# RWKV attention with a top-1 router: attention in halves of 64 rows, both products of R as one moving operand

## The chip, the cores and the metric

One core of a Trainium2 chip. The metric is the device time of one launch in microseconds (us), the median of the runs.

## The reference

Attention (4 sequences, 8 heads, 768 steps, width 48), step by step, and then a router that sends each of 3072 tokens to the best of 8 experts:

```
for t in range(S):
    cur = u * k_t (outer) v_t
    y_t = r_t @ (state + cur)
    state = w * state + k_t (outer) v_t
x = y as [3072, 384];  logits = norm(x) @ norm(emb).T / tau
e = argmax(logits);    gate = softmax(logits)[e]
out = gate * (relu(x @ w1[e]) @ w2[e])          # float32 throughout
```

## The kernel before, in words

The attention is worked in chunks of 128 steps, two sequences at a time: 6 chunks x 2 pairs of sequences = 12 *turns* (t = 0 to 11; `c, bp = divmod(t, 2)`). After the turns come the experts, one after the other, which the change does not touch except for the names of two PSUM banks.

In a chunk K and R are scaled by powers of w that grow and fall with the row (`scale_k`, `scale_r`, GpSimd). TensorE turns them so that the width lies on partitions (`turn_in`, L304) and ScalarE copies them out of PSUM (`take_in`, L308: tiles KT, RT). `scores` (L318) multiplies 128 rows of K with 128 rows of R for each of 16 heads (8 heads, 2 sequences, u = 0 and 1; `par` is the head's parity and chooses a bank and 64 of the 128 partitions). VectorE multiplies with a triangle (`mask`, L350: tile AT). The diagonal carries the extra factor u: GpSimd makes KT times u (`own_k`, L286: tile KuT), TensorE makes the diagonal blocks of 64 x 64 from it (`own_scores`, L333) and VectorE writes their diagonals into AT (`own_terms`, L342). `outer` (L363) adds the chunk's K and V to the state (`next_state` L375, `decay_state` L381 on GpSimd). One turn later `with_state` (L399) and `with_v` (L412) make Y, ScalarE takes it out (`take_y`), TensorE turns it (`turn_y`, L427), ScalarE copies X out of PSUM, stores it by DMA and sums its squares.

Each second turn a chunk of four sequences is complete, and its routing follows as the *lists' steps*: `logits` (L453, TensorE), `take_logits` (lgT), `turn_logits`, `keep_logits` (lg), `choose` (L490 to L503, VectorE, with the norms' powers by GpSimd, L482), `exps`, `ranks` (TensorE), `places`, `gate`, `places_b` (tiles HV, QV, P on VectorE, L553 to L564), `put` (L572, TensorE) and `collect` (lists). The experts gather their rows by these lists.

All engines take their instructions in order. The order is written by hand: `attention` gives each step a planned time, `plan.at(time, step)`, and the steps are emitted in the order of these times. PERIOD is the planned length of a turn, 11.2; the times set only the order. PSUM has 8 banks: ps0 to ps3 (`k.D`), po0 and po1 (`k.O`), py0 and py1 (`k.Y`). The line that ties GpSimd's product to the scores is in `own_k`: `after(k, ins, k.scored)`.

Of the kernel before, what the change touches and what calls it, by code (L numbers as in the profile page):

```python
# [19 lines left out]
C = 128  # L20
NCH = S // C
# [12 lines left out]
PERIOD = 11.2  # L34
# [33 lines left out]
def build_first(k):  # L68
# [23 lines left out]
    step = k.AT[1][:, 0, 0].rearrange("q (p i) -> q p i", p=NP)  # L92
    seed = k.AT[1][:, 0, 1].rearrange("q (p i) -> q p i", p=NP)
# [18 lines left out]
    for src, dst, bank in ((kp, k.kpow, k.O[0]), (rp, k.rpow, k.O[1])):  # L112
# [27 lines left out]
def build_consts(k):  # L140
# [8 lines left out]
    k.dmask = k.aconst.tile([128, DP], I32, name="dmask")  # L149
    for s in range(2):  # L150
        q = slice(s * DP, (s + 1) * DP)
        nc.vector.tensor_copy(k.dmask[q, :], k.ident[q, q])
# [73 lines left out]
def rings(k):  # L226
# [54 lines left out]
def scale_r(k, t, u):  # L281
    k.nc.gpsimd.tensor_mul(of(k.Rw, t)[:, u, :, 0:D], of(k.R, t)[:, u], k.rpow)  # L282


def own_k(k, t, u):
    ins = k.nc.gpsimd.tensor_mul(  # L286
        of(k.KuT, t)[:, u], of(k.KT, t)[:, u], k.uw[:, :, None].to_broadcast([128, NP, C])
    )
    if u == 0:
        after(k, ins, k.scored)  # L290
# [16 lines left out]
def take_in(k, t, u, which):  # L307
    k.nc.scalar.copy(  # L308
        of(k.KT if which else k.RT, t)[:, u], k.turned[u][which].rearrange("q (p i) -> q p i", p=NP)
    )  # L310


def scores(k, t, u):
    RT, KT = of(k.RT, t), of(k.KT, t)
    for p in range(NP):
        for par in range(2):
            rows = slice(par * DP, par * DP + D)
            k.scored = k.nc.tensor.matmul(  # L318
                k.D[2 * u + par][:, p * C : (p + 1) * C], KT[rows, u, p, :], RT[rows, u, p, :],
                start=True, stop=True, skip_group_check=True,  # L320
            )


def own_scores(k, t):

    RT, KuT = of(k.RT, t), of(k.KuT, t)
    for u in range(2):
        for p in range(NP):
            for s in range(2):
                for par in range(2):  # L330
                    rows, half = slice(par * DP, par * DP + D), slice(s * DP, (s + 1) * DP)
                    col = (u * NP + p) * DP
                    k.nc.tensor.matmul(  # L333
                        k.O[par][half, col : col + DP], KuT[rows, u, p, half], RT[rows, u, p, half],
                        start=True, stop=True, skip_group_check=True,
                    )
# [12 lines left out]
def mask(k, t, u, par):
    k.nc.vector.tensor_mul(  # L350
        of(k.AT, t)[:, u, par].rearrange("q (p i) -> q p i", p=NP),
        k.D[2 * u + par].rearrange("q (p i) -> q p i", p=NP),
        k.umask[:, None, :].to_broadcast([128, NP, C]),
    )


def outer(k, t):
    Kw, V = of(k.Kw, t), of(k.V, t)
    for u in range(2):
        for p in range(NP):  # L360
            for par in range(2):
                h, col = 2 * p + par, (u * NP + p) * D
                k.nc.tensor.matmul(  # L363
                    k.sums[par * DP : (par + 1) * DP, col : col + D], Kw[:, u, h, :], V[:, u, h, 0:D],
                    start=True, stop=True, skip_group_check=True,
                )


def next_state(k, t):
    c, bp = divmod(t, 2)  # L370
    new = k.sums[:, 0 : 2 * NP * D].rearrange("q (u p d) -> q u p d", u=2, p=NP)
    if c == 0:
# [11 lines left out]
def y_out(k, par, p, u):  # L384
    col = (u * 2 + p % 2) * C
    return k.Y[par][(p // 2) * DP : (p // 2 + 1) * DP, col : col + C]


def with_state(k, t):
    c, bp = divmod(t, 2)  # L390
    if c == 0:
        return
    RT, T = of(k.RT, t), k.T[bp][c % 2]
    for u in range(2):
        for q in range(2):
            for p in (q, q + 2):
                for par in range(2):
                    rows = slice(par * DP, par * DP + D)
                    k.nc.tensor.matmul(  # L399
                        y_out(k, par, p, u)[0:D], T[rows, u, p, :], RT[rows, u, p, :],  # L400
                        start=u == 0 and q == 0, stop=False, skip_group_check=True,
                    )


def with_v(k, t):
    c, bp = divmod(t, 2)
    AT, V = of(k.AT, t), of(k.V, t)
    for u in range(2):
        for q in range(2):
            for par in range(2):  # L410
                for p in (q, q + 2):
                    k.nc.tensor.matmul(  # L412
                        y_out(k, par, p, u), V[:, u, 2 * p + par, :], AT[:, u, par, p * C : (p + 1) * C],
                        start=c == 0 and u == 0 and q == 0, stop=True, skip_group_check=True,
                    )
# [153 lines left out]
def put(k, c):  # L569
    out = k.Y[1][:, 128 : 128 + 2 * E * TM]  # L570
# [6 lines left out]
def collect(k, c):  # L577
    new = k.Y[1][:, 128 : 128 + 2 * E * TM].rearrange("q (x j t) -> q x j t", x=E, j=2)
# [7 lines left out]
def attention(k):  # L586
# [3 lines left out]
    for t in range(TURNS):  # L590
# [459 lines left out]
```

## Time and profile before

| | |
|---|---|
| median of 3 runs | 560.61 us (560.07 to 563.74) |
| the profiled execution | 561.12 us, its span 559.3 us |
| TensorE granted clock, mean | 0.951 |
| TensorE busy | 502.6 us (90%), 3755 instructions |
| VectorE, ScalarE, GpSimd busy | 154.1, 103.5, 158.8 us |

The profile is of one execution; times are us from the start of its span. A float32 matmul shows as two records, so 16 matmuls are x32. PE is TensorE's matmuls, PEld its weight loads, DVE VectorE, ACT ScalarE, POOL GpSimd, SP the queue that issues most DMAs. A granted clock of 1.00 is TensorE's upper level (2.4 GHz), 0.50 the lower (1.2 GHz).

### The profile page before, as it was taken

The numbers are of one execution on the slowest core, as the hardware profiler recorded it, in microseconds if no ns is written. First come the engines' busy times: TensorE is split into PE (matmuls) and PEld (weight loads), VectorE is DVE, ScalarE is ACT, GpSimd is POOL, SyncE is SP. The second block draws the span as 40 slices with busy tenths as digits, with TensorE's granted clock in tenths as the row PEclk, the third lists the DMA queues.
The fourth block names the chain that finished last, engine by engine and source line by source line (L and its number), as shares of the span: only waits on it lengthen the run. The fifth ranks groups of instructions, "written<-read, shape, count | busy, mean of one in ns | idle before, by whom it ended". The sixth has DMA issues, their size and how long they took to land.

```text
span 559.3 us, 9057 instructions
## 1 busy us (share of the span) xinstructions
PE 502.6 (90%) x3755; PEld 316.6 (57%) x3755; DVE 154.1 (28%) x352; ACT 103.5 (19%) x223; POOL 158.8 (28%) x191
## 2 busy tenths in 40 slices
PE   7588998989897389999999999999999999999990
PEld 3487787878776244554554554554554554554550
DVE  6545667685772310200200110110110110100001
ACT  1123444333342102002002002002002102101100
POOL 5545656465640360130131031022013010020010
PEclk9788999999996679999999999999999999999996
DMA  8925579995000130341332322313314313010010
GB/s 170 198 50 124 116 163 253 281 233 125 31 31 28 51 100 0 128 142 41 128 112 76 128 88 93 127 57 129 126 34 154 113 42 113 0 44 0 0 41 8
DMA packets 95510, 54.20 MB, mean 97 GB/s; under 512 B 78781, under 2 KB 90110, under 8 KB 95458
## 3 DMA queue, kind: packets, MB, share of 16 engines
q1 hardware_dynamic: 88658, 43.67, 28.2%
q0 software_dynamic: 4096, 9.45, 4.7%
q10 hardware_dynamic: 2704, 0.40, 0.4%
q8 instruction: 31, 0.51, 0.4%
q14 instruction: 21, 0.17, 0.1%
HBM read 45.63 MB, written 11.01 MB: 101 GB/s over the span
## 4 chain that ended last, share of the span: by engine, by line
PE 77%; POOL 7%; DVE 6%; issue 3%; ACT 1%; DMA 1%; POOLq 0%; ACTq 0%; DVEq 0%
PE ps L706 30%; PE po L717 30%; POOL KuT L286 4%; PE ps L318 4%; PE py L412 3%; PE ps L304 2%; DVE AT L342 2%; PE py L697 2%; PE py L572 1%; PE po L333 1%; PE py L453 1%; PE ps L363 1%; DVE xTe L698 1%; POOL Rw L282 1%; POOL Kw L278 1%
## 5 line engine op out<-in xcount | busy, mean ns | idle before, releaser
L706 PE MATMUL ps<-xTe,w 128*128 128x512 f32 x384 | 167.9, 597 | 0.0
L717 PE MATMUL po<-w,hT 128*128 128x384 f32 x512 | 166.4, 486 | 0.0
L717 PEld LDWEIGHTS po<-w,hT 128*128 128x128 f32 x512 | 96.7, 190 | 66.2 <-issue 0.5
L706 PEld LDWEIGHTS ps<-xTe,w 128*128 128x128 f32 x384 | 73.6, 192 | 91.0 <-issue 89.1
L723 POOL DMA_INDIRECT out_dram<-y,take x32 | 31.7, 991 | 281.7 <-DVE y L722 277.5
L709 ACT ACTIVATE hT<-ps 128x512 f32<-128x512 f32 x64 | 38.2, 597 | 300.4 <-PE ps L706 300.4
L722 DVE TENSOR_SCALAR y<-po,lists 128x384 f32<-128x384 f32 x32 | 19.8, 618 | 165.5 <-PE po L717 165.5
L698 DVE COPY xTe<-py 128x512 f32<-128x512 f32 x24 | 15.9, 689 | 153.2 <-PE py L697 153.1
L286 POOL TENSOR_TENSOR KuT<-KT,uw 128x512 f32<-128x512 f32 x24 | 24.5, 1040 | 64.6 <-PE ps L318 61.1
L342 DVE COPY_PREDICATED AT<-dmask,po 64x512 f32<-64x512 int32 x48 | 35.4, 738 | 17.3 <-PE po L333 16.6
L684 POOL DMA_INDIRECT G<-xs,take x32 | 32.6, 1018 | 15.3 <-issue 8.2
L350 DVE TENSOR_TENSOR AT<-ps,umask 128x512 f32<-128x512 f32 x48 | 29.8, 683 | 15.8 <-PE ps L318 15.8
L318 PE MATMUL ps<-RT,KT 48*128 48x128 f32 x384 | 25.1, 281 | 3.0 <-ACT X L431 2.8
L412 PE MATMUL py<-AT,V 128*64 128x128 f32 x384 | 26.6, 297 | 0.0
L419 ACT COPY YT<-py 128x512 f32<-128x512 f32 x24 | 12.9, 589 | 71.0 <-PE py L412 71.0
L318 PEld LDWEIGHTS ps<-RT,KT 48*128 48x128 f32 x384 | 22.8, 190 | 5.6 <-ACT X L431 4.4
L282 POOL TENSOR_TENSOR Rw<-R,rpow 128x384 f32<-128x384 f32 x24 | 24.2, 1007 | 6.1 <-DVE wC L118 5.8
L333 PE MATMUL po<-RT,KuT 48*64 48x64 f32 x768 | 16.7, 224 | 9.8 <-POOL KuT L286 9.8
L278 POOL TENSOR_TENSOR Kw<-K,kpow 128x384 f32<-128x384 f32 x24 | 24.2, 1008 | 0.0
L412 PEld LDWEIGHTS py<-AT,V 128*64 128x64 f32 x384 | 23.5, 150 | 1.1 <-issue 0.4
L697 PE MATMUL py<-ident,G 128*128 128x128 f32 x96 | 15.6, 298 | 8.0 <-DMA G<-xs,take 5.5
L333 PEld LDWEIGHTS po<-RT,KuT 48*64 48x64 f32 x768 | 13.4, 134 | 14.3 <-POOL KuT L286 14.3
(145 smaller groups left out, 339.3 us busy)
## 6 DMA issues: line engine op xcount, KB each, us to landing
w<-in_moe_w_dram SPq DMA_DIRECT2D x24, 512.0 KB, 5.2
w<-in_moe_w_dram SPq DMA_DIRECT2D x32, 384.0 KB, 4.0
K<-in_k_dram SPq DMA_DIRECT2D x24, 192.0 KB, 3.7
V<-in_v_dram SPq DMA_DIRECT2D x24, 192.0 KB, 4.1
xs<-X SPq DMA_DIRECT2D x24, 192.0 KB, 2.0
R<-in_r_dram SPq DMA_DIRECT2D x22, 192.0 KB, 4.0
G<-xs,take POOLq DMA_INDIRECT x32, 3.4
out_dram<-y,take POOLq DMA_INDIRECT x32, 2.6
```

Source lines behind the costliest of these rows:

```text
L278: k.nc.gpsimd.tensor_mul(of(k.Kw, t)[:, u, :, 0:D], of(k.K, t)[:, u], k.kpow)
L286: ins = k.nc.gpsimd.tensor_mul(of(k.KuT, t)[:, u], of(k.KT, t)[:, u], k.uw[:, :, None].to_broadcast([128, NP, C]))
L318: k.scored = k.nc.tensor.matmul(k.D[2 * u + par][:, p * C : (p + 1) * C], KT[rows, u, p, :], RT[rows, u, p, :], start=True, stop=True, ski ...
L333: k.nc.tensor.matmul(k.O[par][half, col : col + DP], KuT[rows, u, p, half], RT[rows, u, p, half], start=True, stop=True, skip_group_check= ...
L342: k.nc.vector.copy_predicated(of(k.AT, t)[half, :, par].rearrange("q u (p i) -> q u p i", p=NP)[:, :, :, half], k.dmask[half, None, None, ...
L350: k.nc.vector.tensor_mul(of(k.AT, t)[:, u, par].rearrange("q (p i) -> q p i", p=NP), k.D[2 * u + par].rearrange("q (p i) -> q p i", p=NP), ...
L412: k.nc.tensor.matmul(y_out(k, par, p, u), V[:, u, 2 * p + par, :], AT[:, u, par, p * C : (p + 1) * C], start=c == 0 and u == 0 and q == 0, ...
L684: k.nc.gpsimd.indirect_dma_start(out=G[:, :], out_offset=None, in_=k.xs[:, :], in_offset=IndirectOffsetOnAxis(ap=k.take[:, e, t : t + 1], ...
L706: k.nc.tensor.matmul(ps, w1[:, m, f * 128 : (f + 1) * 128], xT[:, m, :], start=(m == 0), stop=(m == NK - 1))
L709: k.nc.scalar.activation(hT[:, f, :], ps, ACT.Relu)
L717: k.nc.tensor.matmul(ps, hT[:, f, t * 128 : (t + 1) * 128], w2[:, f, :], start=(f == 0), stop=(f == NF - 1))
L723: k.nc.gpsimd.indirect_dma_start(out=k.out[:, :], out_offset=IndirectOffsetOnAxis(ap=k.take[:, e, t : t + 1], axis=0), in_=y[:, :], in_off ...
```

## The change

The chunk of 128 stays for the scaling and the turning in, but scores, diagonal and state are worked in two halves s of 64 rows:

- RT has two parts side by side for each half: R (copied by ScalarE as before) and R times u (`own_r`, VectorE, reads the turned R in PSUM). `scores` multiplies a half of K (64 columns of weights) with the 128 columns [R, R times u] of the same half: 32 matmuls on four tiles of 64 x 64. `own_k` and `own_scores` are gone, and KuT with them.
- `mask` and `own_terms` read the two parts of one result: 4 instructions of 128x256 each instead of 4 of 128x512 and 4 of 64x512.
- `outer` gives the sums of both halves (32 matmuls, banks pu0 and pu1, which were po0 and po1); `half_state` makes the state in the middle of the chunk (tile Tmid), `next_state` the one at its end.
- Y is made by `with_v` in two phases of 16 matmuls of 64x64 and by `with_state` with 32 matmuls of 64 columns, the second half of them with Tmid. In the first phase row half s writes bank s, in the second bank 1-s; `between` (two copies of one column by ScalarE) stands before the second.
- `scale_r` of turn t+1 now has the tie to the scores of turn t that `own_k` had.
- X is turned through pu0 and pu1; the small results of the lists' steps move from py1 to columns 384 to 511 of these banks. The lists' steps are spread over one turn more, and PERIOD is 9.4.

```diff
+HC = C // 2
-PERIOD = 11.2
+PERIOD = 9.4
 def scale_r(k, t, u):
-    k.nc.gpsimd.tensor_mul(of(k.Rw, t)[:, u, :, 0:D], of(k.R, t)[:, u], k.rpow)
-def own_k(k, t, u):
...
-    if u == 0:
+    ins = k.nc.gpsimd.tensor_mul(of(k.Rw, t)[:, u, :, 0:D], of(k.R, t)[:, u], k.rpow)
+    if t and u == 0:
         after(k, ins, k.scored)
...
+def own_r(k, t, u):
+    k.nc.vector.tensor_mul(
+        of(k.RT, t)[:, u, :, :, 1, :], k.turned[u][0].rearrange("q (p s i) -> q p s i", p=NP, s=2),
+        k.uw[:, :, None, None].to_broadcast([128, NP, 2, HC]),
+    )
 def scores(k, t, u):
...
+        for s in range(2):
+            for par in range(2):
...
+                    k.D[2 * u + par][halves(s), p * C : (p + 1) * C], KT[rows, u, p, halves(s)],
+                    RT[rows, u, p, s].rearrange("q j i -> q (j i)"),
...
+def half_state(k, t):
...
+        k.nc.vector.tensor_add(k.T1[bp], k.T[bp][c % 2], added(k, 0))
 def next_state(k, t):
...
+    k.nc.vector.tensor_add(k.T[bp][(c + 1) % 2], k.T1[bp], added(k, 1))
...
+def between(k, t):
+    for par in range(2):
+        col = (1 - par) * HC
+        k.nc.scalar.copy(k.peek[:, par : par + 1], k.Y[par][:, col : col + 1])
+def with_v(k, t, phase):
...
+                for s in range(2):
+                    par = s if phase == 0 else 1 - s
...
+            plan.at(then + 4.65, keep_logits, k, c)
...
+            plan.at(then + 4.65, placed, k, c)
...
+                plan.at(then + 8.8, places_b, k, c)
+                plan.at(then + P + 1.77, put, k, c)
...
-    plan.at(6.2, build_embeddings, k)
+    plan.at(6.6, build_embeddings, k)
```

Three places show how the order moves. The first is TensorE in a turn that has `put`, from the scores to the second turning in, before (turn 6): rows of one kind show the first of them only.

```order
L318 MATMUL ps_58<-RT_118,KT_121 128x128
L399 MATMUL py_64<-RT_120,T_1_132 48x128
L333 MATMUL po_62<-RT_118,KuT_122 64x64
L412 MATMUL py_64<-AT_123,V_110 64x128 x2
L363 MATMUL ps_58<-V_112,Kw_116 64x48 x16
L304 MATMUL ps_59<-ident,Rw_102 128x128 x4
```

and in the changed kernel (turn 7; `put` is L596, `with_v` L414, `with_state` L433, `outer` L363):

```order
L328 MATMUL ps_60<-RT_119,KT_121 64x128 [waits DVE_49,Activation_49]
L596 MATMUL pu_63<-QV,P 128x64 [waits DVE_49,Activation_49]
L414 MATMUL py_64<-AT_122,V_110 64x64
L433 MATMUL py_64<-RT_118,T_1_131 48x64
L302 MATMUL ps_58<-ident,Rw_102 128x128 [waits DVE_49,Pool_49]
L414 MATMUL py_65<-AT_122,V_110 64x64 [waits Activation_49]
L363 MATMUL pu_62<-V_112,Kw_116 64x48 [waits DMAHW4_49,DVE_49]
L302 MATMUL ps_60<-ident,Rw_102 128x128 [waits Pool_49]
L448 MATMUL pu_62<-ident,YT_124 128x128 [waits DVE_49,Activation_49]
```

`put` has moved from the end of a turn to directly behind the scores, the turning in is split around the second phase of `with_v`, and `outer` now stands behind a wait for VectorE.

The second is VectorE around `places_b` (HV, QV, P) before, where the next masks come behind the copies lgT and lg:

```order
L375 TENSOR_TENSOR T_1_132<-T_0_131,ps_58 128x384 [waits PE_49,Pool_49]
L553 TENSOR_TENSOR HV<-over,ng 128x32
L558 TENSOR_TENSOR QV<-HV,cum_oh 128x256 [waits DVE_49]
L564 TENSOR_TENSOR P<-slot,lo 128x512
L461 COPY lgT<-py_64 128x128 [waits PE_49,Activation_49]
L470 COPY lg<-py_65 128x32 [waits PE_49,Activation_49]
L583 TENSOR_TENSOR lists<-lists,py_65 128x64
L350 TENSOR_TENSOR AT_124<-ps_58,umask 128x512 [waits PE_49,Activation_49]
```

and in the changed kernel:

```order
L567 TENSOR_TENSOR over<-slot,hi 128x16
L482 COPY lgT<-py_64 128x128 [waits PE_49]
L535 TENSOR_REDUCE g<-l 128x4
L536 TENSOR_SCALAR g<-g 128x4 [waits DVE_49]
L537 RECIPROCAL ng<-g 128x4 [waits DVE_49]
L577 TENSOR_TENSOR HV<-over,ng 128x32 [waits DVE_49]
L582 TENSOR_TENSOR QV<-HV,cum_oh 128x256 [waits DVE_49]
L588 TENSOR_TENSOR P<-slot,lo 128x512
L342 TENSOR_TENSOR AT_123<-ps_58,smask 128x256 [waits PE_49]
```

HV, QV and P now stand behind lgT, which waits for the logits at the end of a turn, and directly ahead of the masks of the next turn.

The third is VectorE from the masks to the next turn's R times u in the changed kernel (before, the masks were followed by `own_terms` and `next_state` alone):

```order
L349 COPY_PREDICATED AT_123<-dmask,ps_61 128x256
L315 TENSOR_TENSOR RT_118<-ps_58,uw_192 128x8x64 [waits Activation_49]
L607 TENSOR_TENSOR lists<-lists,pu_63 128x64
L491 COPY lg<-pu_62 128x32
L379 TENSOR_TENSOR Tmid_135<-T_0_132,pu_62 128x384 [waits PE_49]
L384 TENSOR_TENSOR T_1_133<-Tmid_135,pu_63 128x384 [waits DVE_49,PE_49]
L315 TENSOR_TENSOR RT_118<-ps_60,uw_192 128x8x64 [waits Activation_49]
```

`own_r` (L315) stands in VectorE's queue twice in a turn, and lg, which reads the bank that `outer` writes, stands behind the first of them.

## Rows read from the trace of the kernel before

**Rows 1.** The page's first line.

```profile
span 559.3 us, 9057 instructions
```

**Rows 2.** Windows: turns 4, 5 and 6, from scores to scores.

```profile
core 0: us, PE busy (x) PEld busy (x) DVE busy (x) ACT busy (x) POOL busy (x), PEclk, DMA share, GB/s
71.41:84.07 12.66, 12.10 (x258) 10.97 (x258) 8.16 (x18) 5.77 (x15) 7.40 (x9) 1.00 0.80 184
84.07:96.80 12.73, 11.02 (x222) 9.62 (x221) 9.74 (x25) 4.68 (x14) 8.68 (x11) 1.00 0.92 240
96.80:109.53 12.73, 12.17 (x259) 11.04 (x259) 8.16 (x18) 5.84 (x15) 6.68 (x7) 1.00 1.00 280
```

**Rows 3.** The chain that ended last, in turn 4: start, us, what.

```profile
73.65 2.05 POOL KuT L286 x2
75.74 0.69 PE po L333 x32
...
80.27 1.01 PE py L453 x32
...
81.87 0.44 PE po L304 x4
...
83.18 0.84 PE py L572 x8
```

**Rows 4.** Timeline of turn 4, weight loads: start, length, engine, line.

```profile
71.41 1.86 PEld L318 LDWEIGHTS ps<-RT,KT 48*128 48x128 f32 x32 [0.88 <-ACT X L431]
73.39 0.83 PEld L399 LDWEIGHTS py<-RT,T 48*48 48x48 f32 x32
74.74 0.56 PEld L333 LDWEIGHTS po<-RT,KuT 48*64 48x64 f32 x32 [0.51 <-POOL KuT L286]
76.36 1.73 PEld L412 LDWEIGHTS py<-AT,V 128*64 128x64 f32 x32
78.06 1.07 PEld L363 LDWEIGHTS ps<-V,Kw 128*64 128x64 f32 x32
```

**Rows 5.** Groups by form, turns 4 to 9: busy us, mean ns | idle before.

```profile
L342 DVE COPY_PREDICATED AT<-dmask,po 64x512 f32<-64x512 int32 x24 | 17.8, 740 | 8.3 <-PE po L333 8.0
L350 DVE TENSOR_TENSOR AT<-ps,umask 128x512 f32<-128x512 f32 x24 | 14.9, 684 | 4.2 <-PE ps L318 4.2
L375 DVE TENSOR_TENSOR T<-T,ps 128x384 f32<-128x384 f32 x6 | 3.3, 554 | 0.2
```

**Rows 6.** Timeline: one step of choose beside GpSimd, and alone.

```profile
67.25 1.01 POOL L278 TENSOR_TENSOR Kw<-K,kpow 128x384 f32<-128x384 f32 x1
67.48 0.83 DVE L492 TENSOR_TENSOR l<-lg,mx 128x32 f32<-128x32 f32 x1
...
167.79 0.19 DVE L492 TENSOR_TENSOR l<-lg,mx 128x32 f32<-128x32 f32 x1
```

**Rows 7.** Timeline of turn 0: norms of the embeddings, outer, next scores.

```profile
24.02 0.58 POOL L200 TENSOR_TENSOR emb_nrm<-emb_nrm,half 8x1 f32<-8x1 f32 x1
...
27.38 1.95 PE L363 MATMUL ps<-V,Kw 128*64 128x48 f32 x32
...
32.87 2.24 PE L318 MATMUL ps<-RT,KT 48*128 48x128 f32 x32
```

**Rows 8.** Windows of 4 us, PE alone: busy, granted clock, DMA share, GB/s.

```profile
24.00:28.00 4.00, 1.63 (x19) 0.50 1.02 199
...
44.00:48.00 4.00, 2.93 (x40) 1.00 0.49 137
48.00:52.00 4.00, 3.36 (x86) 0.79 0.81 162
```

**Rows 9.** Timeline: first and last scores, and the finished lists.

```profile
15.78 2.25 PE L318 MATMUL ps<-RT,KT 48*128 48x128 f32 x32
...
159.52 2.06 PE L318 MATMUL ps<-RT,KT 48*128 48x128 f32 x32
...
191.53 0.18 DVE L581 TENSOR_TENSOR lists<-lists,py 128x32 f32<-128x32 f32 x1
```

More of the change, by code (lines that the diff above doesn't have):

```diff
@@ L250, in rings @@
     k.T = [[pool.tile([128, 2, NP, D], F32, name=f"T{bp}_{i}") for i in range(2)] for bp in range(2)]
+    k.T1 = [pool.tile([128, 2, NP, D], F32, name=f"Tmid{bp}") for bp in range(2)]
+    k.peek = pool.tile([128, 2], F32, name="peek")
     k.sq = ring("sq", 1, [128, DM])
@@ L569, in put @@
 def put(k, c):
-    out = k.Y[1][:, 128 : 128 + 2 * E * TM]
+    out = k.U[1][:, 384 : 384 + 2 * E * TM]
     for b in range(B):
@@ L604, in attention @@
+            plan.at(before + 4.0 + 2.6 * u, own_r, k, t, u)
             plan.at(at + 0.9 * u, scores, k, t, u)
             for par in range(2):
-                plan.at(at + 1.0 + 1.4 * u + 0.7 * par, mask, k, t, u, par)
-        plan.at(at + 3.2, own_scores, k, t)
-        for par in range(2):
-            for s in range(2):
-                plan.at(at + 4.4 + 1.4 * par + 0.7 * s, own_terms, k, t, par, s)
-        if c < NCH - 1:
-            plan.at(at + 6.4, outer, k, t)
-            plan.at(at + 7.4, next_state, k, t)
-            plan.at(nxt + 7.0, decay_state, k, t)
@@ L615, in attention @@
-        plan.at(nxt + 2.0, with_state, k, t)
-        plan.at(nxt + 4.4, with_v, k, t)
-        for par in range(2):
-            plan.at(nxt + 6.4 + 0.6 * par, take_y, k, t, par)
+                plan.at(at + 0.9 + 1.5 * u + 0.36 * par, mask, k, t, u, par)
+                plan.at(at + 1.65 + 1.5 * u + 0.4 * par, own_terms, k, t, u, par)
+        plan.at(at + 4.75, outer, k, t)
+        plan.at(at + 5.6, half_state, k, t)
+        if c < NCH - 1:
+            plan.at(at + 6.2, next_state, k, t)
+            plan.at(at + 6.8, decay_state, k, t)
@@ L633, in attention @@
-            plan.at(then + 9.72, ranks, k, c)
-            plan.at(then + 9.8, places, k, c)
-            plan.at(then + 11.0, gate, k, c)
-            last = 7.9 if c < NCH - 2 else 0.0
-            plan.at(then + P + last, places_b, k, c)
-            plan.at(then + P + (10.5 if c < NCH - 2 else 0.2), put, k, c)
-            plan.at(then + P + (11.0 if c < NCH - 2 else 0.3), collect, k, c)
-    end = NCH * 2 * P + 6.4
-    c = NCH - 1
-    plan.at(end + 1.3, logits, k, c)
-    plan.at(end + 1.4, take_logits, k, c)
@@ L644, in attention @@
-    plan.at(end + 5.0, turn_logits, k, c)
-    plan.at(end + 5.1, keep_logits, k, c)
-    plan.at(end + 5.9, choose_a, k, c)
-    for i, fn in enumerate((choose, exps, ranks, places, gate, places_b, put, collect)):
-        plan.at(end + 6.0 + i, fn, k, c)
+            plan.at(then + 1.78, turn_logits, k, c)
+            plan.at(then + 4.65, keep_logits, k, c)
+            plan.at(then + 6.9, choose_a, k, c)
+            plan.at(then + 7.5, choose, k, c)
+            plan.at(then + 9.0, exps, k, c)
@@ L649, in attention @@
+    end = NCH * 2 * P + 6.0
+    c = NCH - 1
+    for i, fn in enumerate((
+        logits, take_logits, turn_logits, keep_logits, choose_a, choose, exps, ranks, placed, places, gate,
+        places_b, put, collect,
+    )):
+        plan.at(end + (1.7 if i < 4 else 3.5) + 0.1 * i, fn, k, c)
     plan.at(-P + 0.4, load_small, k)
-    plan.at(6.2, build_embeddings, k)
-    plan.at(P + 6.2, decays, k)
+    plan.at(6.6, build_embeddings, k)
+    plan.at(P + 6.9, decays, k)
     for i, G in enumerate(k.G):
-        plan.at((2 + i // 2) * P + 7.5, k.nc.gpsimd.memset, G, 0.0)
+        plan.at((2 + i // 2) * P + 6.85, k.nc.gpsimd.memset, G, 0.0)
@@ L993 @@
     n.D = [psum.tile([128, 512], F32, name=f"ps{i}") for i in range(4)]
-    n.O, n.Y = ([psum.tile([128, 512], F32, name=f"{x}{i}") for i in range(2)] for x in ("po", "py"))
-    n.bank = [*n.D, *n.O, *n.Y]
-    n.turned = ((n.D[1], n.D[2]), (n.D[3], n.O[0]))
-    n.rows, n.sums = (n.D[0], n.O[1]), n.D[0]
+    n.U, n.Y = ([psum.tile([128, 512], F32, name=f"{x}{i}") for i in range(2)] for x in ("pu", "py"))
+    n.bank = [*n.D, *n.U, *n.Y]
+    n.turned = ((n.D[0], n.D[1]), (n.D[2], n.D[3]))
+    n.rows = n.U
     n.const = pool("const", 1)
```

197 lines of the change are left out of this document (98 added, 99 removed).

## The prediction

> **What bounds the kernel now.** I read the page first: the span is 559.3 us [rows 1], and TensorE is busy nearly throughout, which says nothing yet of what a stage waits for. The attention is the stretch that the change touches: its first scores start at 15.78, its lists are finished at 191.7 [rows 9], and the 368 us of the experts behind that are taken over unchanged. So I predict when the lists are finished. Next come the windows by turn: 12.66 and 12.73 us alternate, TensorE is busy for 12.1 and 11.0 us of them, VectorE for 8.2 and 9.7, at a clock of 1.00, the upper level [rows 2]. The chain says what TensorE waits for: after the scores comes GpSimd's KuT, 2.05 us, and `own_scores` can follow only half by half [rows 3]; `with_state` covers about half of that wait. The timeline of weight loads gives TensorE's prices, since loads start one behind the other where the matmuls' records overlap [rows 4]. So a turn is TensorE's sum plus some 0.6 to 1.7 us of waiting, and VectorE has 3 to 4.5 us to spare.
>
> **TensorE's work in a turn.** Prices come from the spacing of loads, two records to a matmul. A record of 128 columns on four tiles costs 0.83/32 = 26 ns (L399), on tiles two at a time 1.86/32 = 58 ns (L318) and 1.73/32 = 54 ns (L412); a record of 64 columns on four tiles 0.56/32 = 17.5 ns (L333); `outer` pays 1.07/32 = 33 ns [rows 4]. After the change the scores have 64 records of 128 columns: 1.7 us. `with_state`, `outer` and the two phases of `with_v` have 64, 64 and 2 x 32 records of 64 or fewer columns on four tiles: 1.12, 1.12 and 2 x 0.56. The last three kinds have no row of their own; the bounds are 17.5 (nearest in shape) and 33 ns, and I take 17.5. Turning in and out stays at 0.44 for four [rows 3], six times: 2.6. Together 7.6, where the same steps before have 1.86 + 0.83 + 1.12 + 1.73 + 1.07 + 2.6 = 9.2. At each change of tile shape I add 0.1 (the first load of L399 comes 0.12 behind the last of L318 [rows 4]), five of them; then `put` 0.84 and a small turning in turns that have them, `logits` 1.0 [rows 3] and `ranks` 0.6 in the others. That makes 9.3 and 9.7 us.
>
> The Trainium skill has a rule against such splitting: in TensorEngine Tiling (Array Packing), Performance Considerations, every matmul carries about 60 cycles of overhead, and a factor should not be taken from a dimension that is already small. At 2.4 GHz that is 25 ns; by it the 192 records of 64 columns in a turn cost 1.4 us more and the sum comes to 549. The row with 17.5 ns disagrees with it for four tiles side by side; the other kinds are open until they run.
>
> **VectorE's work in a turn.** A mask of 512 takes 0.684 us, an `own_terms` of 512 0.740 [rows 5]. For 256 the bounds are half of that and all of it; I take 0.36 and 0.42, near the half, since the same engine's 384 take 0.554 [rows 5]. Four of each are 3.1 us. `own_r` reads 512 from PSUM like a mask, 0.62 from start to start, twice; the two states 0.5 each. That is 5.4 us, where before it was 6.2. With all eight masks and `own_terms` at the full price the finished lists come 20 us later, which is the outer end. The lists' steps are as they were, about 2.1 and 3.2 us a turn. So VectorE has 7.5 and 8.6 us in a turn that TensorE could do in 9.5, and it now stands three times on TensorE's path: `own_r` before the next scores, lg or the rank before `outer` (the wait in the order), and the states before turning Y.
>
> **A turn walked through.** Both engines in order, each step at its price, from the first scores at 0. In a turn with `put`, VectorE still has lgT (behind the logits), the gate, HV, QV and P before it. HV is done at 1.2. QV and P read two tiles in SBUF, and GpSimd starts Rw and Kw at 1.1, when the first half of the scores is done. A step of that kind took 0.83 us where GpSimd's Kw ran until 68.26, and 0.19 alone [rows 6]; so I let QV and P each end with one of GpSimd's products: P at 3.5 instead of 2.4. `put`, which stands right behind the scores, waits from 1.7 to 3.6. After it, `with_v` and `with_state` end at 6.5, `turn_in` u=0 runs to 7.4; the masks run from 3.5 to 6.6; ScalarE copies RT, `own_r` from 7.9 to 8.5, lists and lg to 8.9. So `outer` starts at 9.0, 0.9 us late; the sums go through `turn_in` u=1, both states (to 11.4) and Y; the next scores start at 12.1. In a turn with `ranks`, VectorE has `choose` first, whose last step waits for the norms by GpSimd and once for Rw: the masks begin at 2.5, the rank is read at 6.7, `outer` starts 1.1 us late, logits end at 10.8: 10.8, or 11.5 where two memsets of G stand ahead of the norms on GpSimd (turns 4 and 6). By the same prices and rules the turns of before come to 12.6 each.
>
> On the price of two SBUF inputs the Trainium skill says more: SBUF — State Buffer, SBUF: two separate sides, has VectorE and GpSimd share a port pair as an exclusive lock, so that whichever starts first keeps it for its whole instruction. The trace agrees for a VectorE step that starts second (0.83 against 0.19 us). Without it the sum would be 4.4 us lower, 533.
>
> **The sum.** Turn 0 takes 11.2 instead of 17.1: GpSimd, without KuT, has the norms of the embeddings (0.58 at 24.02) 1.4 us earlier, and `outer` and the turning in, which filled 27.38 to 32.87 behind them [rows 7], now lie ahead of that wait. Turn 1 is TensorE's sum alone with half the state (7.5), turn 2 has logits (8.6), turn 3 the whole state and the first wait of `outer` (9.2). Turns 4 to 10 are 11.5, 12.1, 11.5, 12.1, 10.8, 12.1 and 10.2 (nothing turned in for a turn 12). From 15.7 that leads to the scores of turn 11 at 132.5. Turn 11 takes 9.4, the last Y with the lists of chunk 4 and the last logits 7.4, the last lists 8.1, a chain of small steps on VectorE that is as before: 157.4, at the upper clock throughout.
>
> The clock comes on top. After TensorE had been busy for 1.63 us of 4 it stood at 0.50, the lower level, and after 2.93 of 4 it fell to a mean of 0.79 in the next 4 us [rows 8]; before's 191.7 is 8 us above its own walk for such stretches (turns 0 and 2 and the end). For after I take 3 us behind the norms in turn 0, 3 at the end, and 4 among the turns, whose TensorE is now busy for 80% with pauses of 1.9: 10 us, so 167.4. The gain is 24 us, and 561.1 - 24 = 537 for the profiled execution, which lies 0.5 us above the median of its runs, so I leave it at 537.
>
> Loads are costed at nothing: turns 4 to 8 moved some 14 MB, at up to 280 GB/s with the DMA engines at a share of 1.00 [rows 2]; at that rate they fill 51 us, and the five turns have 58. A load has two turns between issue and use. Were turns shorter than 10.2, the loads would set them. ScalarE's two copies in `between` (0.2 each) lie beside `turn_in` u=0.
>
> **Rivals.**
> - *VectorE keeps up.* If lg, rank and P come in time, TensorE's sum sets turns 4 to 10: about 9.7 instead of 11.5, 13 us less, 524. For it speaks VectorE's spare time in rows 2; against it, that the order puts P between the logits and the masks.
> - *Small records cost more.* With `with_v` and `outer` at 33 ns, as `outer` pays now [rows 4], the lists come 16 us later: 553; at 25 ns, 549.
> - *The lower clock decides: slower.* Pauses of 1.9 us behind the scores and 1 us at `outer` could keep TensorE at 0.50. A turn of 9.5 us of work then takes 9.5 more, of which some 2.5 go into the waits: 7 us a turn. From three and a half such turns on the gain is gone; if all of turns 4 to 10 run so, 586. Rows 8 show a fall after less pausing than this; against it, turns at 87% busy kept 1.00 [rows 2].
> - *Some of it.* Three turns at the lower clock, or masks of 256 at the full price with the small records dearer: within 1%.
>
> **How the numbers follow.** The forecast, 537, has 0.55; VectorE keeping up 0.20; dear records 0.12; within 1% 0.06; the lower clock 0.07. About 1% is what a measurement of this kernel can tell from no change. So faster 0.87, same 0.06, slower 0.07. The range runs from 518 (the first rival with few stretches of low clock) to 553 (the second in full); what lies above it is the last two.
>
> **What would show it.** Right: turns of 10.8 to 12.1; PE waiting for VectorE's P ahead of `put` (about 1.9) and for lg or the rank ahead of `outer` (about 1); no wait of PE for GpSimd but in turn 0; loads of the new matmuls 17 to 18 ns apart, of the scores 26; a mask near 0.42 and an `own_terms` near 0.48 us busy; turn 0 near 11 to 14. Wrong: no such waits (first rival), spacings of 25 to 33 (second), a granted clock of 0.50 in the middle turns (third), or scores waiting for RT.

## The result and the profile after

Before 560.5 us (560.1 to 563.7, 4 runs), after 531.4 us (530.1 to 535.0, 4 runs): a ratio of 0.948, interval 0.942 to 0.954. The profiled execution of after took 535.0 us, the slowest of its four. The forecast was 537, range 518 to 553.

The page's first lines of after: the span, and the queue that carries instructions (packets, MB, share of 16 DMA engines).

```profile
span 533.2 us, 10611 instructions
q8 instruction: 37, 0.61, 0.5%
```

The span is 26.1 us shorter than in [rows 1]. The lists are finished at 165.8 where before had 191.7 [rows 9], 25.9 us earlier: so all of the gain lies ahead of the experts, as it was meant. The windows of after by turn, from scores to scores (columns as in [rows 2]): turns 0 and 1, turns 4 to 7, and turn 11 to the finished lists. Turns 2, 3, 8, 9 and 10 took 8.49, 11.25, 11.46, 12.65 and 10.14.

```profile
core 0: us, PE busy (x) PEld busy (x) DVE busy (x) ACT busy (x) POOL busy (x), PEclk, DMA share, GB/s
16.42:29.85 13.43, 9.54 (x151) 8.49 (x151) 7.87 (x19) 3.25 (x7) 5.90 (x8) 0.63 0.97 191
29.85:39.50 9.65, 9.65 (x250) 9.04 (x249) 5.51 (x14) 3.64 (x9) 4.46 (x5) 0.77 0.13 26
...
59.24:69.74 10.50, 9.95 (x318) 8.79 (x317) 8.29 (x27) 6.62 (x20) 7.09 (x11) 1.00 0.84 202
69.74:83.84 14.10, 11.04 (x293) 9.55 (x289) 8.04 (x21) 4.37 (x12) 5.15 (x5) 0.88 0.85 217
83.84:94.76 10.92, 9.81 (x318) 8.67 (x317) 8.30 (x27) 6.52 (x20) 6.96 (x10) 1.00 0.83 211
94.76:107.46 12.70, 11.17 (x293) 10.03 (x289) 8.10 (x22) 4.34 (x12) 5.13 (x5) 0.87 0.91 244
...
141.71:165.81 24.10, 16.24 (x438) 14.11 (x434) 14.50 (x63) 7.94 (x28) 2.63 (x4) 0.89 0.14 52
```

Turns 4 to 10 took 88.1 us before (71.41 to 159.52) and take 82.5 now: 5.6 us of 25.9. Turn 11 with the end of the lists gives 8.1 (32.2 against 24.1), turns 0 to 3 12.8 (55.6 against 42.8), and the first scores start 0.6 later. In the odd turns 5, 7 and 9, which have `put`, the clock is no longer 1.00, as it was in [rows 2], but 0.87 or 0.88: in this execution part of each ran at the lower level.

What TensorE waited for in turns 3 to 9 of after (us in total, times, longest), and then the longest such row in turns 2 to 9 of before:

```profile
PE ps L302 <- issue: 3.2, 2, 2.1
PE pu L596 <- DVE P L588: 2.7, 3, 1.2
PE pu L363 <- DVE full L550: 1.5, 3, 0.6
PE py L433 <- issue: 1.1, 1, 1.1
PE pu L363 <- DVE lg L491: 1.0, 2, 0.6
PE pu L363 <- issue: 0.9, 1, 0.9
```

```profile
PE po L333 <- POOL KuT L286: 5.5, 16, 1.3
```

The waits for KuT are gone, and the forecast's two are there: `put` (L596) for P, `outer` (L363) for lg and the rank. But "issue" was no wait of the forecast, and before has no such row in these turns. It is time in which TensorE waited for nothing that the profile shows. Weight loads in after's timeline, turns 3 and 5:

```profile
51.07 0.23 PEld L433 LDWEIGHTS py<-RT,Tmid 48*48 48x48 f32 x9
52.56 0.40 PEld L433 LDWEIGHTS py<-RT,Tmid 48*48 48x48 f32 x23 [1.26 <-issue]
...
75.94 0.14 PEld L302 LDWEIGHTS ps<-ident,Kw 128*128 128x128 f32 x1
78.45 0.36 PEld L302 LDWEIGHTS ps<-ident,Kw 128*128 128x128 f32 x3 [2.36 <-issue]
```

TensorE stops in the midst of a step: 9 of 32 loads of `with_state` are done, the other 23 come 1.26 us later, though they read the same tiles and write the same banks. In this profile there are four such pauses longer than 0.35 us in turns 2 to 10, 5.0 us in all; the other two are in the scores of turn 5 (0.91) and in `with_v` of turn 7 (0.47). In before there is only the 0.44 us in `own_scores`, which is the wait for KuT's second half. I call them *pauses in a step*, and count them in the same way below.

What the DMA queues show beside them: in this run and those below, each pause ends 1.2 to 1.65 us behind the end of a packet of 16 KB on q8. For the first, the windows of the DMA queues 49.5 to 51.2 of after hold that packet (packets, MB, share), with the loads at 91% of all DMA engines; in 51.2 to 52.56 there is no packet of q8.

```profile
q1 hardware_dynamic: 1129, 0.37, 91.2%
q8 instruction: 1, 0.02, 5.5%
```

That q8 carries TensorE's instructions shows in its volume first. It moved 0.61 MB for 9046 records of TensorE here and 0.51 MB for 7510 before, 67 and 68 bytes a record. The row of before's page:

```profile
q8 instruction: 31, 0.51, 0.4%
```

It shows in the places of the pauses, too. Ahead of the four pauses TensorE's loads, matmuls and sequencer have 1729, 2754, 3009 and 4289 records in the trace: these counts lie 1025, 255 and 1280 apart, multiples of 256 within one, and 256 records of 64 bytes are one packet of 16,384 bytes. All 72 pauses in turns 2 to 10 of the changed kernel and of the edits below lie at such an end of a *block* of 256 records. So in a pause TensorE waits for the packet with its next block.

The theory for the experiments was: the forecast's waits on VectorE are real, but TensorE now also uses up its instructions faster (21 such packets between the scores of turns 2 and 11, 4.9 us apart, where before had 16, 7.2 us apart). Where loads fill the DMA engines, the next ones come late.

### The profile page after: what moved, and what is told of

It reads as the page before. It is cut to its first block, busy times and chain, and to the rows that moved or that the text cites. A ratio compares the mean times of both kernels' runs of the same rounds, so it can differ in the third digit from the quotient of the medians.

```text
span 533.2 us, 10611 instructions
## 1 busy us (share of the span) xinstructions
PE 483.6 (91%) x4523; PEld 299.4 (56%) x4523; DVE 143.9 (27%) x390; ACT 106.2 (20%) x247; POOL 137.5 (26%) x167
## 4 chain that ended last, share of the span: by engine, by line
PE 79%; DVE 8%; issue 3%; POOL 1%; DMA 1%; ACT 1%; POOLq 0%; DVEq 0%; ACTq 0%
PE ps L733 31%; PE pu L744 31%; PE ps L302 3%; PE pu L363 2%; PE py L724 2%; PE py L414 2%; PE ps L328 2%; PE py L433 2%; PE pu L448 1%; PE pu L596 1%; PE py L474 1%; DVE P L588 1%; DVE xTe L725 1%; DVE AT L342 1%; DVE RT L315 1%
## 5 line engine op out<-in xcount | busy, mean ns | idle before, releaser
L744 PE MATMUL pu<-w,hT 128*128 128x384 f32 x512 | 166.4, 486 | 0.0
L744 PEld LDWEIGHTS pu<-w,hT 128*128 128x128 f32 x512 | 96.7, 190 | 66.2 <-issue 0.5
L749 DVE TENSOR_SCALAR y<-pu,lists 128x384 f32<-128x384 f32 x32 | 19.7, 617 | 165.5 <-PE pu L744 165.5
L328 PE MATMUL ps<-RT,KT 48*64 48x128 f32 x768 | 27.8, 297 | 0.8 <-issue 0.7
L328 PEld LDWEIGHTS ps<-RT,KT 48*64 48x64 f32 x768 | 24.3, 148 | 3.3 <-issue 2.7
L302 PE MATMUL ps<-ident,Rw 128*128 128x128 f32 x96 | 17.4, 306 | 3.7 <-POOL Rw L286 2.1
L315 DVE TENSOR_TENSOR RT<-ps,uw 128x512 f32<-128x512 f32 x24 | 16.4, 687 | 13.5 <-ACT RT L309 13.4
L724 PEld LDWEIGHTS py<-ident,G 128*128 128x128 f32 x96 | 11.7, 149 | 14.6 <-DMA G<-xs,take 6.5
L414 PE MATMUL py<-AT,V 64*64 64x64 f32 x768 | 18.8, 238 | 1.0 <-ACT peek L402 0.6
L342 DVE TENSOR_TENSOR AT<-ps,smask 128x256 f32<-128x256 f32 x48 | 17.8, 410 | 4.9 <-PE ps L328 4.9
L363 PE MATMUL pu<-V,Kw 64*64 64x48 f32 x704 | 15.6, 235 | 3.9 <-DVE full L550 2.0
```

The costliest lines, as they stand in the source:

```text
L302: k.nc.tensor.transpose(bank[:, p * C : (p + 1) * C], pair(src[:, u], p), k.ident)
L328: ins = k.nc.tensor.matmul(k.D[2 * u + par][halves(s), p * C : (p + 1) * C], KT[rows, u, p, halves(s)], RT[rows, u, p, s].rearrange("q j i ...
L363: k.nc.tensor.matmul(k.U[s][par * DP : (par + 1) * DP, col : col + D], Kw[halves(s), u, h, :], V[halves(s), u, h, 0:D], start=True, stop=T ...
L414: k.nc.tensor.matmul(y_out(k, par, p, u, s), V[halves(s), u, 2 * p + par, :], AT[halves(s), u, par, p * HC : (p + 1) * HC], start=first an ...
L724: k.nc.tensor.transpose(ps[:, t * 128 : (t + 1) * 128], G[:, m * 128 : (m + 1) * 128], k.ident)
L744: k.nc.tensor.matmul(ps, hT[:, f, t * 128 : (t + 1) * 128], w2[:, f, :], start=(f == 0), stop=(f == NF - 1))
```

## The experiments

All times are to be read against the changed kernel, 531.4 us at first and 534.6 in `again`, where single executions went from 530 to 537.

**again**: the changed kernel, unedited.

> The changed kernel once more, as the standard for the runs beside it. Both theories: the same as its first measurement, 530 to 535 us, lists finished at 163 to 167. Open question: whether the pauses inside TensorE's stream that no semaphore explains (1.3 and 0.9 us in turn 3, 0.9 and 2.4 us in turn 5 of the first profile) come at the same places again.

534.6 us (531.8 to 537.2), ratio 0.953 (0.947 to 0.959); lists at 163.9. Six pauses in a step, 8.7 us. All four of the first profile come again in the same steps (`with_state` at 51.7, scores at 71.1, turning Kw at 77.6, `with_v` at 103.5), so their place belongs to the program, but their lengths are 0.7, 1.2, 2.6 and 2.7; two are new. Turn 9, without pause and at a clock of 1.00, took 11.15. Of the odd turns only turn 7 ran in part at the lower level (0.88).

**lgT_behind_P**

> VectorE's copy of the logits (lgT) goes behind gate, HV, QV and P instead of ahead of them; nothing else moves. Theory of the prediction (P is late because VectorE has lgT, which waits for the logits, before it, and because GpSimd's products run beside it): P starts about 1 us earlier, put no longer waits for it, and turns 5, 7 and 9 are about 1 us shorter each: lists 3.3 us earlier, 528 us. Rival (something else, loads or the clock, sets those turns): put's wait goes, but the time stays within 1 us of the changed kernel.

```diff
-            plan.at(nxt + 8.6, take_logits, k, c)
+            plan.at(nxt + 8.85, take_logits, k, c)
```

530.6 us, ratio 0.943 (0.939 to 0.948); lists at 166.5. Groups by form of turns 3 to 9, P in after and then P here:

```profile
L588 DVE TENSOR_TENSOR P<-slot,lo 128x512 f32<-128x512 f32 x3 | 4.5, 1484 | 0.0
```

```profile
L588 DVE TENSOR_TENSOR P<-slot,lo 128x512 f32<-128x512 f32 x3 | 2.1, 684 | 0.0
```

P is done when GpSimd's Rw starts, or has started before it (turn 5), takes 0.68 us instead of 1.48, and no row of `put` waiting for P is left. But the pauses took its place. What TensorE waited for most here, turns 3 to 9:

```profile
PE py L433 <- issue: 3.7, 3, 2.0
PE ps L302 <- issue: 2.7, 2, 1.4
```

Ten pauses in a step, 10.0 us, and turn 6, in which three of them fall and the lower clock follows, took 18.2. Turn 9 shows the exchange: it has no wait for P and a clock of 1.00, but `with_state`, whose first records stand at the end of a block, starts 1.07 us late, and the turn takes 11.25 where `again` has 11.15. So to take the wait for P away was worth what the theory says only if nothing stood behind it. The rival's number came true for the lists; the median is 4 us below `again`, with intervals that just overlap.

**early_lg**

> VectorE's copy of the turned logits (lg), the reading of the ranks (full, rank) and the adding to the lists go between the first two own_terms, right behind what they read, instead of behind the first own_r. Theory of the prediction (outer waits 0.4 to 1 us in each turn from 3 on for these steps, since they read the banks that outer writes): outer's wait goes and turns 3 to 10 are 0.7 to 1 us shorter, lists 7.8 us earlier, 523 to 524 us. Rival (the masks, the states or own_r are next in line right away): 0 to 2 us.

```diff
-            plan.at(then + 4.65, keep_logits, k, c)
+            plan.at(then + 1.95, keep_logits, k, c)
-            plan.at(then + 4.65, placed, k, c)
+            plan.at(then + 1.95, placed, k, c)
-                plan.at(then + P + 4.64, collect, k, c)
+                plan.at(then + P + 1.94, collect, k, c)
```

531.6 us, ratio 0.947 (0.942 to 0.951); lists at 164.3. In turns 8 to 10, nearly without pauses and with no wait of `outer` left, it shows 9.9, 10.5 and 9.5, where `again` has 10.3, 11.15 and 10.1: 0.3 to 0.7 a turn, as `outer`'s wait goes. In turns 3 to 8 seven pauses, 8.7 us, all but one of them ahead of turn 8, took it back. Half a hit: the wait is there and goes, with somewhat less than the 0.7 to 1 us a turn, but by the total the rival's 0 to 2 us came true.

**norms_later**

> The embeddings' norms are computed where they were, but TensorE turns them one turn later (in turn 1, before Y is turned), so that the scores of turn 1 don't stand behind them. Theory of the prediction (turn 0 of 11 us includes a wait of 3 us for the norms, which before was longer behind KuT): scores of turn 1 start 3.5 us earlier than 29.85, lists 2.8 us earlier plus 1 to 2 us of low clock in turn 1: 527 to 529 us. Rival (the rows of turn 1 aren't ready, so it waits as long for RT or the state): lists at most 1 us earlier.

```diff
     plan.at(6.6, build_embeddings, k)
+    plan.at(P + 6.64, turn_embeddings, k)
```

(`turn_embeddings` is the second half of `build_embeddings`, from the transposes on; the scaled rows wait in YT2.) In after, TensorE stands at the embeddings; timeline of TensorE, turn 0:

```profile
28.06 0.59 PE L216 MATMUL py<-ident,YT 8*128 8x8 f32 x4 [3.04 <-DVE YT L209]
29.47 0.45 PE L224 MATMUL ps<-ident,X 8*128 8x8 f32 x3 [0.82 <-DVE X L220]
29.86 3.46 PE L328 MATMUL ps<-RT,KT 48*64 48x128 f32 x54
```

Here the scores of turn 1 follow at once:

```profile
20.52 0.60 PE L307 MATMUL ps<-ident,Kw 128*128 128x128 f32 x4
21.05 1.10 PE L333 MATMUL ps<-RT,KT 48*64 48x128 f32 x32
```

Turn 0 took 6.0 instead of 13.4 (11.9 in `again`), turn 1 10.4; the lists were done at 155.8, 8 us earlier than in `again`, and TensorE's granted clock was 1.00 in turns 0 and 1, where after had 0.63 and 0.77. Six pauses, 8.0 us. 530.6 us as a median of four, ratio 0.946 (0.941 to 0.950). The profiled execution is the fastest of its four (525.7), so the 8 us, more than the theory's 2.8, are its own; by the medians it is 4 us below `again`, with intervals that overlap.

**few_loads**

> K, R and V are loaded for turns 0 to 3 only and their old contents used again after that, so turns 4 to 11 compute with wrong data; the experts' weights and X's stores stay. Open since the runs before: pauses of TensorE in the midst of a step (5 to 10 us a run in turns 2 to 8), each ending 1.3 to 1.6 us behind a packet of 16 KB on the queue that carries TensorE's instructions. Theory A (the instructions come late because the loads fill the DMA queues): the pauses in turns 3 to 8 fall to under 2 us, turns 5 to 8 become 10.3 to 11.2, lists at 153 to 157. Theory B (64 columns a record use instructions faster than they can be brought, loads or not): the pauses stay at 5 us and more, lists at 162 or later.

```diff
-        if t:
+        if 0 < t < 4:
             plan.at(at - 3 * P + 0.5, load, k, t, slice(0, 2))
```

531.2 us in the one execution. One pause in a step is left, 2.9 us at 89.4, behind 8 us with weights and stores of X at 264 to 355 GB/s; in turns 2 to 5 there is none, though weights moved there too (312 GB/s from 56 to 60). Turns 3, 7, 8, 9 and 10 took 9.2, 11.15, 10.5, 11.1 and 10.1. By the pauses that is nearer to theory A (the loads hold the instructions up), though A had asked for under 2 us. By the lists, done only at 162.2, it is theory B's number, since the pause at 89.4 and the lower clock behind it made turn 6 16.3 long, and turn 5 ran at a lower clock for a part (12.6) with no pause, behind `put`'s wait.

**weights_later**

> The loads of the first two experts' weights (6 MB) are issued from turn 7 and turn 10 on instead of turns 4 and 6, so that they come beside fewer loads of K, R and V. Theory A: pauses of TensorE in the midst of a step under 4 us in all, lists 4 to 7 us earlier, 524 to 528 us. Theory B: no change of the pauses, 530 to 535 us. If the experts wait for weights, TensorE shows it behind the lists.

```diff
-            plan.at((4 + 2 * e) * P + 1.0 + i * 4.0, piece)
+            plan.at((7 + 3 * e) * P + 1.0 + i * 4.0, piece)
```

533.1 us, ratio 0.950 (0.946 to 0.955). Four pauses, 5.0 us, two of them now in turns 9 and 10 (at 121.5 and 132.5), which had the weights' loads instead. So two of the pauses went with the loads; A's 524 to 528 us didn't come, and moving the weights alone gains nothing that can be told.

**lists_as_before**

> The changed attention with the lists' steps where the kernel before had them, scaled to the shorter turn: the logits turned right behind themselves, choose and ranks one turn earlier, P and put at the end of the following turn. So put doesn't wait for P, but TensorE waits for lgT in turns 2, 4, 6, 8 and 10 and for choose ahead of the ranks. By the prediction's prices: turns 3 to 10 of 10.2 and 11.2 instead of 11.5 and 12.1, lists 1.4 us earlier: within 2 us of the changed kernel, 529 to 533 us. If the new spread is what makes the gain, it is 8 us or more slower.

```diff
-            plan.at(then + 1.78, turn_logits, k, c)
+            plan.at(nxt + 8.9, turn_logits, k, c)
...
-                plan.at(then + P + 1.77, put, k, c)
+                plan.at(then + P + 8.8, put, k, c)
```

(All twelve of the lists' times go back, in proportion; for chunk 4, `put` stands ahead of the last `with_v`.) 545.8 us, ratio 0.972 (0.968 to 0.977): 11 us above `again`, where I had expected none. The profiled execution, at 540.4 the shortest of its four, shows 6.7 of them. Their place is the end: from the scores of turn 11 to the lists 30.8 us instead of 24.1. Timeline of TensorE there:

```profile
148.50 0.40 PE L544 MATMUL pu<-counts,ones 128*128 128x32 f32 x2
152.07 1.94 PE L596 MATMUL pu<-QV,P 128*128 128x64 f32 x8 [3.18 <-DVE P L588]
153.94 1.13 PE L414 MATMUL py<-AT,V 64*64 64x64 f32 x32
```

TensorE stands 3.2 us for P with the last `with_v` behind it, and then runs that at the lower clock (`put` 1.94 for 1.10). In the changed kernel the last `with_v` and `with_state` lie between the ranks and `put`, whose wait there is 0.54. Its turns 0 to 10 took 124.7 us, with six pauses of 10.0 us in all, those of after 125.3. So by the medians the new spread of the lists' steps is worth some 11 us of the 27 to 29 gained, and I had not priced it apart. Without it the change still gains 15 us (545.8 against 560.9 for before beside it).

**four_moves** (lgT_behind_P, early_lg, norms_later and weights_later together)

> lgT behind P, lg and ranks read early, the embeddings turned a turn later and the weights loaded later, all in one. If the prediction's waits and the late instructions are all there is: the three gains of 3.3, 7.8 and 2.8 us by the prices, and the pauses gone; lists at 148 to 152, 515 to 519 us. If the pauses only grow where the waits were (as they did with lgT behind P): lists at 155 or later, 522 us or more.

528.1 us (524.1 to 531.8), ratio 0.942 (0.937 to 0.948); six pauses, 8.0 us. The lists were done at 155.1, but from the scores of turn 11 on it took 26.4 instead of 24.1, with the weights' loads beside it at up to 315 GB/s. That is the second expectation, by the lists and by the time: the pauses grow where the waits were.

**five_moves**: as four_moves, but with the first expert's weights from turn 8 on and the second's behind the last X, and R's load behind V's.

> lgT behind P, lg and ranks read early, the embeddings turned a turn later; R's load issued behind V's (which waits for a buffer until the middle of a turn) instead of ahead of it, so that stores of X, K, weights and R don't start in one go; the first expert's weights from turn 8 on and the second's behind the last X. Theory A (late instructions behind bursts of loads): pauses of TensorE in the midst of a step under 4 us in turns 2 to 8, lists at 148 to 153, 516 to 522 us, below four_moves. If the pauses only move: 524 to 531 us.

```diff
-            plan.at(at - 3 * P + 0.5, load, k, t, slice(0, 2))
-            plan.at(at - 3 * P + 5.0, load, k, t, slice(2, 3))
+            for i, when in enumerate((0.5, 6.0, 5.0)):
+                plan.at(at - 3 * P + when, load, k, t, slice(i, i + 1))
...
+            plan.at((8 * P + 1.0, TURNS * P + 9.0)[e] + i * (4.0, 0.5)[e], piece)
```

522.1 us (517.7 to 524.0, 6 runs), ratio 0.927 (0.923 to 0.930): the fastest here that leaves nothing out, some 10 us below the changed kernel, and clear of both its intervals. But eight pauses are left, 9.5 us, four of them in turns 8 and 9 with the weights: so the gain is not for the reason that I gave, or not for it alone, and which of the moves brings it stays open.

**three_moves_few_loads**

> lgT behind P, lg and ranks read early, the embeddings turned later, with K, R and V loaded for turns 0 to 3 only (wrong data after that) and the weights loaded behind the last X: the prediction's prices with late instructions left out. By them turns 3 to 10 are 8.5, 10.5, 10.2, 10.5, 10.2, 9.8, 10.2 and 9.2 where the changed kernel has 9.2, 11.5, 12.1, 11.5, 12.1, 10.8, 12.1 and 10.2; lists at 148 to 151 with the low clock of turn 1 and of the end. If the waits of put and outer were covered by something else that comes next: turns 3 to 10 within 0.4 us of those of few_loads without pauses (9.2, 11.1, 11.2, 10.5, 11.1, 10.1). The experts then wait for weights, so its total isn't compared.

Pauses in a step 2.0 us; lists at 147.5. What TensorE did in turns 5, 7 and 9, which have `put`:

```profile
64.40:74.00 9.60, 9.37 (x293) 8.35 (x289) 7.09 (x21) 4.39 (x12) 4.61 (x5) 1.00 0.12 44
85.70:94.90 9.20, 9.20 (x298) 8.32 (x293) 7.11 (x21) 4.47 (x13) 4.58 (x5) 1.00 0.13 46
104.80:113.90 9.10, 9.10 (x293) 8.35 (x289) 7.06 (x20) 4.26 (x13) 4.61 (x5) 1.00 0.13 47
```

TensorE is busy with hardly a gap at a clock of 1.00, in 9.1 to 9.6 us. That is the forecast's own sum of 9.3 for such a turn, and 2 us less than turns 7 and 9 of few_loads: with P and lg in time and the instructions too, nothing else comes next there. Turn 6, with a pause of 1.3 us, took 11.7.

**few_loads_R_by_GpSimd**

> few_loads with one part of the change undone: R times u is made by GpSimd from the copy in SBUF instead of by VectorE from PSUM. By the rows, GpSimd takes 1.0 us for 128x512 where VectorE takes 0.69, twice a turn, and VectorE has 1.4 us less to do. If VectorE's place on TensorE's path is what sets the turns: turns 7 to 10 up to 0.7 us shorter than in few_loads (11.15, 10.5, 11.1, 10.1). Rival: GpSimd, which also has Rw, Kw, the state and the norms, comes late with RT or the norms, and turns are 0.3 to 1 us longer.

```diff
-    k.nc.vector.tensor_mul(
-        of(k.RT, t)[:, u, :, :, 1, :], k.turned[u][0].rearrange("q (p s i) -> q p s i", p=NP, s=2),
+    k.nc.gpsimd.tensor_mul(
+        of(k.RT, t)[:, u, :, :, 1, :], of(k.RT, t)[:, u, :, :, 0, :],
```

Timeline of turn 7: GpSimd's product, P and `put`.

```profile
94.13 1.04 POOL L315 TENSOR_TENSOR RT<-RT,uw 128x512 f32<-128x512 f32 x1 [1.95 <-ACT RT L309]
...
98.13 1.47 DVE L588 TENSOR_TENSOR P<-slot,lo 128x512 f32<-128x512 f32 x1
99.75 1.08 PE L596 MATMUL pu<-QV,P 128*128 128x64 f32 x8 [2.09 <-DVE P L588]
```

`put` waits 2.1 instead of 1.2; turns 7, 8 and 10 took 11.6, 10.8 and 10.3, 0.2 to 0.5 longer than in few_loads. The rival's sign at its lower end, 535.1 us against 531.2: VectorE out of PSUM was the better place, by little, as far as one execution of each can tell.

**three_moves**: five_moves with the loads where the changed kernel has them.

> lgT behind P, lg and ranks read early and the embeddings turned a turn later, with all loads where the changed kernel has them: five_moves without its two moves of loads, and three_moves_few_loads with the loads. If the order of the loads matters (theory A): pauses of TensorE in the midst of a step of 8 us or more in turns 2 to 8, lists at 154 to 160, 524 to 530 us. If it doesn't: as five_moves, 520 to 524 us.

525.2 us (523.9 to 529.7, 6 runs), ratio 0.937 (0.933 to 0.941), ten pauses, 12.6 us. Against five_moves the intervals part: the places of the loads are worth 0.6% by the medians and 1.1% by the ratios, where `weights_later` alone showed nothing. Against three_moves_few_loads the lists come 9.3 us later (156.8 to 147.5): the price of the loads, paid in pauses (12.6 us to 2.0). What TensorE waited for most from 42 to 132 us, turns 3 to 10, with the loads (lines are five higher than in after) and then, in the same stretch, without:

```profile
PE ps L307 <- issue: 5.7, 3, 2.3
PE py L438 <- issue: 2.5, 2, 1.4
```

```profile
PE pu L368 <- issue: 1.1, 1, 1.1
PE ps L307 <- issue: 1.0, 2, 0.7
```

## Why the prediction was right, step by step

*TensorE's prices* held. Weight loads of turn 8 in after:

```profile
107.46 1.74 PEld L328 LDWEIGHTS ps<-RT,KT 48*64 48x64 f32 x64 [0.17 <-issue]
...
109.94 0.56 PEld L414 LDWEIGHTS py<-AT,V 64*64 64x64 f32 x32
110.40 0.54 PEld L433 LDWEIGHTS py<-RT,T 48*48 48x48 f32 x32
...
114.87 1.02 PEld L363 LDWEIGHTS pu<-V,Kw 64*64 64x64 f32 x64 [0.54 <-DVE full L550]
```

1.74/64 = 27 ns for the scores (26 forecast), 0.56/32 = 17.5 for `with_v`, 0.54/32 = 17 for `with_state`, 1.02/64 = 16 for `outer` (17.5 forecast, 33 as its upper bound). The rival of dear records falls. The Trainium skill (TensorEngine Tiling (Array Packing), Performance Considerations) states an overhead of about 60 cycles for each matmul, by an estimate from it 25 ns for each record at 2.4 GHz. In four tiles side by side it doesn't show: records of 64 columns and fewer lie 16 to 17.5 ns apart.

*VectorE's prices* held too; groups by form of after, turns 3 to 9:

```profile
L349 DVE COPY_PREDICATED AT<-dmask,ps 128x256 f32<-128x256 int32 x28 | 10.7, 432 | 0.0
L342 DVE TENSOR_TENSOR AT<-ps,smask 128x256 f32<-128x256 f32 x28 | 10.4, 409 | 0.7 <-PE ps L328 0.7
L315 DVE TENSOR_TENSOR RT<-ps,uw 128x512 f32<-128x512 f32 x14 | 9.6, 689 | 11.7 <-ACT RT L309 11.6
```

0.41 and 0.43 us for 256, where 0.42 and 0.48 were to be seen, 0.69 for `own_r`.

*The wait of* `put`: turn 7 of after.

```profile
94.89 0.29 DVE L482 COPY lgT<-py 128x128 f32<-128x128 f32 x1 [0.37 <-PE py L474]
96.00 1.23 POOL L286 TENSOR_TENSOR Rw<-R,rpow 128x384 f32<-128x384 f32 x1 [1.99 <-PE ps L328]
96.30 1.48 DVE L588 TENSOR_TENSOR P<-slot,lo 128x512 f32<-128x512 f32 x1
97.20 1.44 POOL L282 TENSOR_TENSOR Kw<-K,kpow 128x384 f32<-128x384 f32 x1
97.90 0.97 PEld L596 LDWEIGHTS pu<-QV,P 128*128 128x128 f32 x8 [1.41 <-issue]
```

The order is the forecast's: lgT, gate, HV, QV, then P beside GpSimd. `put` starts 3.1 us behind the scores' start instead of 3.6 and so waits 1.4, not 1.9. P, which starts 0.3 us behind Rw, takes 1.48 and ends about half-way through Kw; GpSimd's products grow too, from 1.0 to 1.23 and 1.44. By SBUF — State Buffer, SBUF: two separate sides, of the Trainium skill, the engine that starts first keeps the shared ports; the trace agrees in that P takes 0.68 without GpSimd beside it.

*The wait of* `outer` is 0.54 to 0.70 us where it has one, where I had 0.9 to 1.1. So a turn without pauses and at full clock takes 10.5 (even) and 11.15 (odd), where I had 10.8 to 11.5 and 12.1. This part of the forecast was some 5 us too long over turns 4 to 10.

*Loads are costed at nothing*: this is the step that failed. I had looked only at whether data come in time, and no scores waited for RT. But the loads also stand before TensorE's own instructions, which nothing in before shows. In after that costs 5.0 us within steps, and 2.4 more where a block ends between two steps: turning in at 57.34 and at 113.19 started 1.1 and 1.3 us late, both within two records of such an end (for the second the profile names GpSimd's Kw, but that was done at 111.1). That these are waits for instructions is shown by the count of records. That the loads make the packets late is shown by the runs without most of them, with 0.7 to 2.9 us of pauses in a step, where the kernels with all loads have 5.0 to 12.6; how the queue is served was not tried.

*The clock*: 10 us were set aside. In the odd turns, (1 - 0.875) x 2 is the share at the lower level, 3.2 us of some 13, so 1.6 us of work lost in each: 4.9 us, where 4 stood. That is this execution, the slowest of its four; what makes the clock fall in one turn and not in another stays open, since `again` had it in one odd turn and three_moves, with 12.6 us of pauses, in none of turns 2 to 10. Turns 0 and 1 took 23.1 where 18.7 plus 3 stood, turn 11 and the end 24.1 where 24.9 plus 3 stood.

*The sum*: the scores of turn 11 started at 141.7, where 132.5 plus 7 stood, the lists were done at 165.8 for 167.4. The waits came out shorter, the pauses were added, and the two nearly cancelled: that the total is so near is in part luck. So 537 against 531.4 is a hit of the total, and right in its mechanism for TensorE's and VectorE's work, but not in every term. The rival that VectorE keeps up is what turns 5, 7 and 9 of three_moves_few_loads reach; the lower clock never held a whole turn of the steady ones.

## What to carry to other kernels

A step that is split into more and shorter matmuls needs its instructions faster, and here they came by DMA, late where loads filled the DMA engines: look for pauses in the midst of a step, with no semaphore, count the records between them, and try the loads that aren't urgent elsewhere. After a wait is taken away, ask what stood behind it: two of the edits here removed just the wait that they aimed at and gained little, until they came together with less crowded loads. And price a moved small step by what stands behind it in order on its engine at the end of the program too, where nothing covers it: there the spread of the lists' steps earned 6.7 us in the profiled executions, more than the 5.6 of the whole change in turns 4 to 10.

## What was not expected of the hardware

TensorE's pauses in a step: 0.4 to 2.9 us each, 5 to 13 us in a run, all at the end of a block of 256 records; 2.9, 2.0 and 0.7 us in the three runs without most loads, none in the kernel before. Open is why each ends so steadily 1.2 to 1.65 us behind its packet, and whether the same volume of loads in fewer packets would do less harm.

With a pause or a wait the clock sometimes fell: in few_loads turn 6 TensorE paused 2.9 us, up to 89.4, and stood at 0.50, the lower level, from 88 to 92. There a pause costs more than its length. But in three_moves, with ten pauses of up to 2.4 us, the granted clock was 1.00 in each of turns 2 to 10.
